# Two attention decode blocks on one core: every engine's program as a loop over one unit, with the score product written over the K tile

## The chip, the cores and the metric

The kernel runs on one core of a Trainium2 chip. The metric is the device time of one execution in microseconds, as a median of runs. The engines are TensorE (PE in the profile, with its weight loads as PEld), VectorE (DVE), ScalarE (ACT), GpSimd (POOL) and SyncE (SP), which issues the loads. A "q" behind an engine's name (PEldq, SPq) marks instructions of its queue: register arithmetic, branches, waits and the issue of transfers.

## The reference

Two independent blocks, A and B, of the same form and size. Each has one query token for each of 2 sequences:

```
q      = (x @ wq)                      # x: 2 x 1 x 640, wq: 640 x 6144, 32 heads of 192
scores = q . k_cache * 192 ** -0.5     # k_cache: 2 x 32 x 8192 x 192
p      = softmax(scores)               # over the 8192 keys
o      = p . v_cache                   # v_cache: 2 x 32 x 8192 x 192
out    = o @ wo                        # wo: 6144 x 640
```

The results of A and B are concatenated along the last axis. All data is bf16. The four caches are 805 MB; nearly all bytes are read once and used once.

## The kernel before

The work is cut into 64 units. A unit is a pair of neighbouring heads of one sequence of one block: a K tile and a V tile of 128 partitions x 24,576 bf16 elements (6.29 MB each). Partitions 0 to 63 hold the first head, 64 to 127 the second; a partition holds 128 keys of 192 numbers.

Three buffers in SBUF (`rings`, three slots of `RW` elements) take the tiles in the order K0, V0, K1, V1 and so on, each into the next slot. All loads go through SyncE's queue, in program order. A load waits until its slot is free: a K slot after the unit's fourth product (key `("m", i, 3)`), a V slot after the unit's V product (key `("pv", i)`); a V load waits for the V load before it too.

The steps of unit i:

- VectorE multiplies the K tile by the broadcast query, in four quarters of 32 keys each (`add_mul`, L322). The product goes to one of two buffers `prod`.
- TensorE sums each quarter's product over the 192 numbers in 12 steps of 16, as 12 accumulating matmuls with the identity (`add_sum`, L327), 128x512 into one of two PSUM banks `scps`; VectorE reduces the remaining 16 (`add_red`, L333) into the scores `sc`.
- VectorE takes each head's maximum per partition, GpSimd the maximum over partitions (L342), ScalarE the exponential (L354) into `pb`, with its sum in `rs`.
- TensorE multiplies the weights with the V tile: 64 accumulating matmuls of 34 weight columns by 384 (`add_pv`, L369), and sums `rs` over the partitions with a matmul (`add_l`, L382).
- In the next unit ScalarE and VectorE combine and normalise the two heads' output (`add_od`, `add_on`), and TensorE puts it into its place of the PSUM tile `oall` with 4 small matmuls (`add_place`, L410).
- TensorE broadcasts the query of the unit after next with one matmul (`add_q`, L309), and ScalarE copies it to `qt`, one of three buffers.
- TensorE also runs 12 matmuls on constant data per unit, whose results are not used (`add_fill`, L377).

Ahead of the units come the query projections: for each block 12 chunks of 512 columns, 5 matmuls each (`add_proj`, L291), from wq loaded in pieces into a slot and a `prod` buffer. Behind them comes the output projection: 48 rows per block (`add_contract`, L425), two matmuls a row, into partitions 0 and 32 of `outps`; the block A rows first, then its result is copied out, then block B. wo comes in 3 pieces (A) and 8 pieces (B).

The order on each engine is written out by hand: the class `_Stream` collects an engine's operations with what they wait for, and `loop` emits a stretch of them as a hardware loop. Before the change TensorE's unit is the body of one loop with 64 passes: 130 matmuls written out one after the other. VectorE and ScalarE have three units as a body, 21 passes. The projection is a loop of 6 passes for each block, two chunks a pass. SyncE and GpSimd have no loop. Semaphores count each engine's operations, so in a loop the value to wait for is worked out in a register (L112, L119). The V product's operand is the one of the large groups whose address comes from a register:

```python
at = slot * RW
if t is not None:
    at = eng.snap(((t * 2) % 3) * RW)
for j in range(T // 2):
    ins = eng.matmul(ops[0:34, 0:2 * Dh], pb[:, j, :], rings[:, bass.ds(at + j * (2 * Dh), 2 * Dh)],
                     start=(j == 0), stop=(j == T // 2 - 1))
```

Of the kernel before, what the change touches and what calls it, by code (L numbers as in the profile page):

```python
# [12 lines left out]
class _Stream:  # L13

    def __init__(self, name, sem, reg, first=0):
        self.name = name
        self.sem = sem
        self.reg = reg
        self.first = first
        self.count = first  # L20
        self.ops = []
        self.marks = []

    def add(self, fn, waits=(), sig=None):
        if sig is not None:
            self.count += 1
            assert sig not in self.reg, sig
            self.reg[sig] = (self.sem, self.count)
        self.ops.append((fn, tuple(waits), sig is not None))

    def mark(self):
        self.marks.append(len(self.ops))

    def needs(self, waits):
        need = {}
        for key in waits:
            if key is None or key[1:] and key[0] != "wo" and key[1] < 0 and key not in self.reg:
                continue
            sem, val = self.reg[key]
            sid = id(sem)  # L40
            if sid not in need or need[sid][1] < val:
                need[sid] = (sem, val)
        return need

    def run(self, eng, ops, waited):
        for fn, waits, has_sig in ops:
            for sid, (sem, val) in self.needs(waits).items():
                if val > waited.get(sid, 0):
                    eng.wait_ge(sem, val)  # L49
                    waited[sid] = val  # L50
            if fn is None:
                continue
            ins = fn(eng, None)
            if has_sig:
                ins.then_inc(self.sem, 1)

    def emit(self, eng, *loops, nc=None):
        waited, done = {}, 0
        if self.first:
            eng.sem_inc(self.sem, self.first)  # L60
        if nc is None:
            waited, done = self.rolled(eng, loops, waited, done)
            self.run(eng, self.ops[done:], waited)
            return
        names = [f"{self.name}_{x}" for x in ("main", "close", "end")]
        self.run(eng, self.ops[:1], waited)
        eng.br(names[0])
        marks, i0, step, n = loops[-1]
        with nc.body(names[1], valid_engines=[eng.engine]):
            self.run(eng, self.ops[marks[i0 + step * n]:], {})  # L70
            eng.br(names[2])
        with nc.body(names[0], valid_engines=[eng.engine]):
            self.rolled(eng, loops, waited, 1)
            eng.br(names[1])
        nc.switch_bb(names[2])

    def rolled(self, eng, loops, waited, done):
        for marks, i0, step, n in loops:
            at = [marks[i0 + step * t] for t in range(n + 1)]
            self.run(eng, self.ops[done:at[0]], waited)  # L80
            self.loop(eng, at, n, waited)
            waited, done = {}, at[n]
        return waited, done

    def loop(self, eng, at, n, waited):
        size = at[1] - at[0]
        passes = [self.ops[at[t]:at[t + 1]] for t in range(n)]
        needs = [[self.needs(w) for _, w, _ in ops] for ops in passes]
        delta = [{sid: needs[2][k][sid][1] - val for sid, (_, val) in need.items()} for k, need in enumerate(needs[1])]
        by, early = {}, {}  # L90
        for k, d in enumerate(delta):
            for sid, v in d.items():
                assert by.setdefault(sid, v) == v or not v or not by[sid]
                by[sid] = max(by[sid], v)
            for t, need in enumerate(needs):
                assert len(passes[t]) == size and passes[t][k][2] == passes[0][k][2]
                assert set(need[k]) == set(d) or t == 0 and set(need[k]) < set(d)
                for sid, (sem, val) in need[k].items():
                    plain = needs[1][k][sid][1] + (t - 1) * d[sid]
                    assert val == plain or t == 0 and val > plain  # L100
                    if val > plain:
                        early[sid] = (sem, max(val, early.get(sid, (sem, 0))[1]))
        for sid, (sem, val) in early.items():
            if val > waited.get(sid, 0):
                eng.wait_ge(sem, val)
                waited[sid] = val
        for k, need in enumerate(needs[1]):
            for sid, (sem, val) in need.items():
                if not delta[k][sid] and val > waited.get(sid, 0):
                    eng.wait_ge(sem, val)  # L110
                    waited[sid] = val
        with eng.Fori(0, n) as t:  # L112
            base = {sid: eng.snap(t * d) for sid, d in by.items() if d}
            waited = {}
            for k, (fn, _, has_sig) in enumerate(passes[0]):
                for sid, (sem, val) in needs[1][k].items():
                    at0 = val - delta[k][sid]
                    if delta[k][sid] and at0 > waited.get(sid, 0):
                        eng.wait_ge(sem, base[sid] + at0)  # L119
                        waited[sid] = at0  # L120
                    assert not delta[k][sid] or at0 > 0
                ins = fn(eng, t)
                if has_sig:
                    ins.then_inc(self.sem, 1)


def build_kernel(nc, blocks, out):
# [6 lines left out]
    NP = NBLK * B * PB  # L134
    LAST = NP - 1
    T = 128
    NB = 3
    STEP = 3
    LOOP = (1, STEP, 21)
    FIRST = 64  # L140
    TQ = T // 4
    DG = 16
# [3 lines left out]
    RW = T * Dh  # L146
    QC = 512
# [3 lines left out]
    WA = [(0, 19, 1, 0), (19, 38, 1, 19), (38, 48, 2, 0)]  # L151
    WB = [(0, 14, 2, 10), (14, 24, 2, 24), (24, 32, 0, 0), (32, 38, 0, 8), (38, 43, 0, 14), (43, 46, 0, 19),
          (46, 47, 0, 22), (47, 48, 0, 23)]

    def pair(i):
        blk, r = divmod(i, B * PB)
        b, ii = divmod(r, PB)
        return blk, b, ii

    with ExitStack() as es:  # L160
# [4 lines left out]
        qt = [sb(f"qt{i}", [128, Dh], BF16) for i in range(3)]  # L165
        sc = [sb(f"sc{i}", [128, T], F32) for i in range(NB)]
        filler = sb("filler", [128, 512], BF16)
        sb("spare", [128, 64], F32)
        rings = sb("rings", [128, 3 * RW], BF16)
        ring = [rings[:, i * RW:(i + 1) * RW] for i in range(3)]  # L170
        prod = [sb(f"prod{i}", [128, TQ * Dh], BF16) for i in range(2)]
        qrow = sb("qrow", [34, N], BF16)
        pb = sb("pb", [128, T // 2, 34], BF16)
        mp = [sb(f"mp{i}", [128, 2], F32) for i in range(NB)]
        mg = [sb(f"mg{i}", [128, 2], F32) for i in range(NB)]
        nb = [sb(f"nb{i}", [128, 1], F32) for i in range(NB)]
        rs = sb("rs", [128, 2], F32)
        rc = [sb(f"rc{i}", [2, 1], F32) for i in range(NB)]
        oodd = [sb(f"oodd{i}", [2, Dh], F32) for i in range(NB)]
# [4 lines left out]
        sel = sb("sel", [34, NBLK * B, 128], BF16)  # L184
        place = sb("place", [2, 264], BF16)
        ones = sb("ones", [128, 1], F32)
        oallS = [sb(f"oallS{k}", [128, WR, 2], BF16) for k in range(NBLK)]
        out_sb = [sb(f"out_sb{k}", [34, NH2], BF16) for k in range(NBLK)]
        actd = sb("actd", [128, 2], F32)
        warm = sb("warm", [128, 2], F32)  # L190

        scps = [ps(f"scps{i}", [128, TQ, DG], F32) for i in range(2)]
        ops = ps("ops", [128, 512], F32)
        pps = [ops, ps("pps", [128, 512], F32)]
        qps = ps("qps", [128, 512], F32)
        oall = ps("oall", [128, 512], F32)
        outps = ps("outps", [128, 512], F32)

        reg = {}
        S_sp = _Stream("sp", sem("s_sp"), reg)  # L200
        S_pe = _Stream("pe", sem("s_pe"), reg, FIRST)
        S_act = _Stream("act", sem("s_act"), reg, FIRST)
        S_dve = _Stream("dve", sem("s_dve"), reg, FIRST)
        PASS = [[], []]
        S_pool = _Stream("pool", sem("s_pool"), reg, FIRST)
        rsem = [sem(f"rsem{i}") for i in range(3)]
        psem = [sem(f"psem{i}") for i in range(2)]
        vsem = sem("vsem")
        xsem = sem("xsem")
        osem = [sem(f"osem{k}") for k in range(NBLK)]  # L210
        rcount = [0, 0, 0]

        def load(key, slot, out_ap, in_ap, waits):
# [387 lines left out]
```

## Time and profile before

| | |
|---|---|
| time, median of 3 runs | 1936.77 us (1936.73 to 1937.01) |
| span of the profiled execution, first to last instruction | 1935.5 us |
| busy: PE, DVE, ACT, POOL | 85%, 56%, 10%, 1% |
| DMA queue's share of 16 engines | 99.9% |
| read from HBM | 836.77 MB, 432 GB/s over the span |
| instructions | 26145 |

The profiled execution has no time of its own beside its span; the runs' median is 1.3 us above the span. In the profile a row of a group gives the line, the engine, the operation, the output and input tiles, the shapes, the count, then the busy time and the mean duration in ns, then the engine's idle time before these instructions with what ended it. A row of the timeline gives the start and the duration in us of a run of equal instructions. A row of one source line gives the shortest, median and longest duration in ns and the first and last start in us; the instructions of an engine's queue stand only there. "issue" is idle time in which the engine waited for nothing that the profile shows. A matmul's end is modelled, so rows of matmuls that follow closely overlap.

### The profile page before, as it was taken

How to read it: one execution, taken by the hardware profiler on the slowest of the kernel's cores; microseconds unless marked ns; L12 is line 12 of the kernel's file. 1: busy time of each engine (PE TensorE's matmuls, PEld its weight loads, DVE VectorE, ACT ScalarE, POOL GpSimd, SP SyncE). 2: the span in 40 equal slices, each digit the busy share in tenths (PEclk: the TensorE clock that was granted, in tenths of full speed). 3: DMA queues.
4: the chain of work that ended last, by engine and by line, in shares of the span. 5: the costliest groups of instructions: out<-in, count | busy, mean ns of one | idle time of the engine just before them, and what ended most of it. 6: DMA issues, size and time to landing. Idle time of an engine off the chain costs nothing.

```text
span 1935.5 us, 26145 instructions
## 1 busy us (share of the span) xinstructions
PE 1637.3 (85%) x8653; PEld 791.5 (41%) x8718; DVE 1081.5 (56%) x837; ACT 188.2 (10%) x612; POOL 28.6 (1%) x86
## 2 busy tenths in 40 slices
PE   4888888888888888888888888888888888888888
PEld 1344443443443443443443443443443443443444
DVE  0556646646656646646656646646656646646652
ACT  2111011011011011011011011011011001001000
POOL 1000000000000000000000000000000000000000
PEclk9999999999999999999999999999999999999999
DMA  9999999999999999999999999999999999999999
GB/s 421 431 430 439 435 428 438 437 428 436 437 429 435 438 431 432 439 435 428 438 435 431 435 437 431 433 439 434 429 438 435 430 436 436 431 434 438 431 433 392
DMA packets 20768, 836.87 MB, mean 432 GB/s; under 512 B 2316, under 2 KB 2584, under 8 KB 3096
## 3 DMA queue, kind: packets, MB, share of 16 engines
q1 hardware_dynamic: 20752, 836.78, 99.9%
q8 instruction: 3, 0.05, 0.0%
q14 instruction: 5, 0.04, 0.0%
q10 hardware_dynamic: 8, 0.00, 0.0%
HBM read 836.77 MB, written 0.01 MB: 432 GB/s over the span
## 4 chain that ended last, share of the span: by engine, by line
issue 92%; DMA 3%; PE 3%; POOL 1%; DVE 1%; ACT 0%; SPq 0%; POOLq 0%; DVEq 0%; ACTq 0%
DMA rings<-in_B_wq_dram 2%; POOL mg L342 1%; PE ops L369 1%; DMA rings<-in_B_wo_dram 1%; DVE prod L322 1%; PE scps L327 1%; PE ops L291 0%; PE pps L291 0%; SPq L219 0%; DVE sc L333 0%; ACT pb L354 0%; POOLq L49 0%; ACT qrow L297 0%; DVE mp L339 0%; ACT out_sb L433 0%
## 5 line engine op out<-in xcount | busy, mean ns | idle before, releaser
L322 DVE TENSOR_TENSOR prod<-rings,qt 128x6144 bf16<-128x6144 bf16 x256 | 852.8, 3352 | 698.6 <-DMA rings<-in_B_k_cache_dram 332.3
L327 PE MATMUL scps<-prod,ident 128*128 128x512 bf16 x3072 | 708.7, 381 | 193.5 <-DVE prod L322 193.5
L369 PE MATMUL ops<-rings,pb 128*34 x4096 | 676.5, 326 | 4.9
L327 PEld LDWEIGHTS scps<-prod,ident 128*128 128x128 bf16 x3072 | 280.3, 98 | 598.6 <-DVE prod L322 293.0
L369 PEld LDWEIGHTS ops<-rings,pb 128*34 128x34 bf16 x4096 | 399.4, 98 | 263.7 <-issue 11.2
L333 DVE TENSOR_REDUCE sc<-scps 128x32 f32<-128x512 f32 x256 | 175.7, 686 | 109.2 <-PE scps L327 109.2
L377 PE MATMUL outps<-filler,ident 128*128 128x512 bf16 x704 | 162.4, 379 | 10.2 <-issue 10.2
L377 PEld LDWEIGHTS outps<-filler,ident 128*128 128x128 bf16 x768 | 69.9, 98 | 77.9
L386 ACT ACTIVATE oodd<-ops 2x192 f32<-2x192 f32 x64 | 20.6, 322 | 699.4 <-PE ops L369 699.4
L315 ACT ACTIVATE qt<-qps 64x192 bf16<-64x192 f32 x66 | 21.4, 324 | 670.1 <-PE qps L309 670.1
L354 ACT ACTIVATE pb<-sc,nb 64x128 bf16<-64x128 f32 x128 | 81.5, 636 | 8.0
L382 PE MATMUL ops<-ones,rs 128*2 128x1 f32 x128 | 12.1, 164 | 58.4 <-ACT pb L354 58.4
L342 POOL PARTITION_ALL_REDUCE mg<-mp x64 | 22.8, 356 | 1871.7 <-DVE mp L339 1871.7
L347 ACT ACTIVATE nb<-mg 64x1 f32<-64x1 f32 x64 | 13.0, 203 | 307.9 <-POOL mg L342 307.9
L382 PEld LDWEIGHTS ops<-ones,rs 128*2 128x2 f32 x128 | 5.5, 82 | 90.0 <-ACT pb L354 90.0
L354 ACT ACTIVATION_READ_ACCUMULATOR pb<-sc,nb 64x1 f32 x128 | 38.4, 300 | 0.0
L309 PE MATMUL qps<-qrow,sel 34*128 (+1 forms) x66 | 22.0, 333 | 1.4 <-ACT qt L316 0.8
L410 PEld LDWEIGHTS oall<-on,place 2*128 x260 | 10.5, 92 | 28.6 <-issue 27.1
L338 DVE TENSOR_REDUCE mp<-sc 64x1 f32<-64x128 f32 x64 | 17.8, 278 | 7.9
L316 ACT ACTIVATE qt<-qps 64x192 bf16<-64x192 f32 x66 | 21.5, 326 | 0.8
L392 DVE TENSOR_TENSOR oodd<-ops,oodd 2x192 f32<-2x192 f32 x64 | 20.8, 326 | 0.2 <-ACT oodd L386 0.2
L394 DVE TENSOR_SCALAR on<-oodd,rc 2x192 bf16<-2x192 f32 x64 | 19.7, 307 | 2.3
(53 smaller groups left out, 165.7 us busy)
## 6 DMA issues: line engine op xcount, KB each, us to landing
rings<-in_A_k_cache_dram SPq DMA_DIRECT2D x32, 6144.0 KB, 26.1
rings<-in_A_v_cache_dram SPq DMA_DIRECT2D x32, 6144.0 KB, 28.9
rings<-in_B_k_cache_dram SPq DMA_DIRECT2D x32, 6144.0 KB, 26.1
rings<-in_B_v_cache_dram SPq DMA_DIRECT2D x32, 6144.0 KB, 28.9
rings<-in_A_wq_dram SPq DMA_DIRECT2D x1, 6144.0 KB, 20.7
rings<-in_B_wq_dram SPq DMA_DIRECT2D x1, 6144.0 KB, 37.5
rings<-in_A_wo_dram SPq DMA_DIRECT2D x2, 3040.0 KB, 22.3
rings<-in_B_wo_dram SPq DMA_DIRECT2D x1, 2240.0 KB, 23.2
```

The lines of the kernel that those rows point to most:

```text
L309: return eng.matmul(qps[:, 0:2 * Dh], sel[:].rearrange("p s m -> p (s m)")[:, bass.ds(k, 128)], qrow[:, bass.ds(c, 2 * Dh)], start=True, s ...
L315: eng.activation(qt[i % 3][0:64, :], qps[0:64, 0:Dh], ACTF.Identity)
L316: return eng.activation(qt[i % 3][64:128, :], qps[64:128, Dh:2 * Dh], ACTF.Identity)
L322: S_dve.add(lambda eng, t: eng.tensor_tensor(pr3(qd), quarter(i, qd), q, ALU.mult), waits=w, sig=("m", i, qd))
L327: ins = eng.matmul(scps[qd % 2][:], ident[:], pr3(qd)[:, :, j * DG:(j + 1) * DG], start=(j == 0), stop=(j == NJ - 1))
L333: S_dve.add(lambda eng, t: eng.tensor_reduce(sc[i % NB][:, qd * TQ:(qd + 1) * TQ], scps[qd % 2][:], AXL.X, ALU.add), waits=[("s", i, qd), ...
L342: S_pool.add(lambda eng, t: eng.partition_all_reduce(mg[i % NB][:], mp[i % NB][:], 128, bass.bass_isa.ReduceOp.max), waits=[("mx", i), key ...
L354: ins = eng.activation(pb[p0:p0 + 64, :, h::32], sc[i % NB][p0:p0 + 64, :].rearrange("p (j a) -> p j a", a=2), ACTF.Exp, bias=nb[i % NB][p ...
L369: ins = eng.matmul(ops[0:34, 0:2 * Dh], pb[:, j, :], rings[:, bass.ds(at + j * (2 * Dh), 2 * Dh)], start=(j == 0), stop=(j == T // 2 - 1))
L377: ins = eng.matmul(to, ident[:], filler[:], start=True, stop=True)
L386: S_act.add(lambda eng, t: eng.activation(oodd[i % NB][:], ops[32:34, Dh:2 * Dh], ACTF.Identity), waits=[("pv", i), key("on", i - NB)], si ...
L392: S_dve.add(lambda eng, t: eng.tensor_tensor(oodd[i % NB][:], ops[0:2, 0:Dh], oodd[i % NB][:], ALU.add), waits=[("od", i)], sig=("ad", i))
```

## The change

The class `_Stream` goes. Each engine has a program written out with loops, and the order of the steps in a unit stays nearly as it was.

- **Loops.** All of TensorE's, VectorE's, ScalarE's, GpSimd's and SyncE's programs have one unit as body, 64 passes (SyncE: one V load and one K load, in loops of 30 and 31 passes). TensorE's unit has loops of its own: 4 quarters, in each of them 4 passes of two matmuls with 4 matmuls outside; 12 passes of one filler matmul; 16 passes of four V matmuls. The projection has one chunk a pass, the output projection one row a pass, with a wait in each. Operands in the ring, in `pb`, in `scps` and in `oallS` are addressed from registers.
- **Product over the K slot.** VectorE writes the product where the K tile is; `prod` goes. The K slot is free for the next V load after the unit's fourth sum (semaphore `su`), no longer after its fourth product.
- **Slots** are `SW` = 30,720 elements apart, so that a whole wq or half of wo fits. wq comes in one load per block, A's wo in one load (before: three), B's in eight.
- **One accumulation for the output.** `oallS` holds four columns for each of the 96 rows, two of them zero, and the rows of both blocks accumulate into the same two PSUM banks, partitions 0 to 3. Two engines copy them out, two queues store them. Two matmuls with a zero operand open and close the V product's accumulation, as the loop's body can't carry the flags.
- **Single buffers** for `sc`, `qt`, `mp`, `mg`, `nb`, `rc`, `oodd`. The query is broadcast one unit ahead instead of two, and copied after the unit's exponential.
- A helper `hold` waits on a semaphore and then counts up another; GpSimd passes on the arrival of wq and wo to TensorE.

The diff, cut to its core:

```diff
-        prod = [sb(f"prod{i}", [128, TQ * Dh], BF16) for i in range(2)]
-        rings = sb("rings", [128, 3 * RW], BF16)
+        rings = sb("rings", [128, 3 * SW], BF16)
...
+        def program_sync(eng):
+            for blk in range(NBLK):
+                w = blocks[blk]["wq"].rearrange("(j c) n -> j (c n)", c=DC)
+                eng.dma_start(slot(blk, SW), w).then_inc(Z[f"wq{blk}"], 16)
...
+            load("k", 0, 0, 2)
+            eng.wait_ge(Z["pr"], NQC)
+            load("v", 0, 0, 0)
+            eng.wait_ge(Z["pr"], 2 * NQC)
+            eng.wait_ge(Z["ks"], 16)
+            load("k", 0, 128, 1)
...
+                hold(eng, "vs", w16)
+                hold(eng, "su", w4)
+                load("v", blk_v, v0, sv)
...
+                hold(eng, "ks", k16)
+                hold(eng, "pv", w1)
+                load("k", blk_k, k0, sk)
...
+                def mul(q):
+                    k3 = rings[:, bass.ds(at + q * QW, QW)].rearrange("p (t d) -> p t d", d=Dh)
+                    eng.tensor_tensor(k3, k3, q3, ALU.mult).then_inc(Z["mu"], 1)
...
+                with eng.Fori(0, NQC) as t:
+                    eng.wait_ge(Z["qe"], eng.snap(k * NQC + t + 1))
+                    to, at = eng.snap((t & 1) * 512), eng.snap(k * SW + t * QC)
+                    for c in range(DC):
+                        ins = eng.matmul(pflat[0:4, bass.ds(to, QC)], xT[:, c, :],
+                                         rings[:, bass.ds(at + c * N, QC)], start=(c == 0), stop=(c == DC - 1))
...
+            with eng.Fori(0, NP) as t:
+                u = eng.snap(t + 1)
+                with eng.Fori(0, 4) as q:
+                    n = eng.snap(t * 4 + q + 1)
+                    at = eng.snap(((t * 2 + 2) % 3) * SW + q * QW)
+                    to = eng.snap((q & 1) * 512)
+                    eng.wait_ge(Z["mu"], n)
+                    eng.wait_ge(Z["re"], n)
...
+                    one(at, True)
+                    one(at + DG, False)
+                    with eng.Fori(0, NJ // 2 - 2) as j:
+                        at_j = eng.snap(at + j * (2 * DG))
+                        one(at_j + 2 * DG, False)
+                        one(at_j + 3 * DG, False)
+                    one(at + (NJ - 2) * DG, False)
+                    ins = one(at + (NJ - 1) * DG, False, True)
+                    ins.then_inc(Z["su"], 1)
+                eng.wait_ge(Z["qtd"], u)
+                make_q(u)
+                n = eng.snap((t + (NP - 1)) & (NP - 1))
+                eng.wait_ge(Z["on"], u)
+                put(eng.snap((n & (3 * PB)) * (WR // PB)), eng.snap((PB - (n & (PB - 1))) * 8)).then_inc(Z["pl"], 1)
+                with eng.Fori(0, 12) as _:
+                    eng.matmul(fps[:], ident[:], filler[:], start=True, stop=True)
+                eng.wait_ge(Z["ex"], u)
+                eng.wait_ge(Z["vs"], eng.snap(u * 16))
+                eng.matmul(ops[0:PW, 0:2 * Dh], zero[:], filler[:, 0:2 * Dh], start=True, stop=False)
...
+                with eng.Fori(0, T // 8) as g:
+                    aj, vj = eng.snap(g * (4 * PW)), eng.snap(g * (4 * 2 * Dh) + sv)
+                    for j in range(4):
+                        eng.matmul(ops[0:PW, 0:2 * Dh], pflat2[:, bass.ds(aj + j * PW, PW)],
+                                   rings[:, bass.ds(vj + j * (2 * Dh), 2 * Dh)], start=False, stop=False)
+                eng.matmul(ops[0:PW, 0:2 * Dh], zero[:], filler[:, 0:2 * Dh], start=False, stop=True)
+                eng.matmul(ops[0:2, 448:449], rs[:], ones[:], start=True, stop=True).then_inc(Z["pv"], 1)
...
+            with eng.Fori(0, NR - PIECES[-1]) as r:
+                eng.wait_ge(Z["wo"], eng.snap(r + 1))
+                contract(r, False, False)
```

In it `one` is a sum's matmul, which takes its operand from the ring at the register's offset and writes to one of the two banks of `scps`, `put` the four matmuls of place, and `contract` a row's two matmuls.

More of the change, by code (lines that the diff above doesn't have):

```diff
@@ L10 @@
 F32 = mybir.dt.float32
[L13 to L124, printed above, removed]
```

594 lines of the change are left out of this document (264 added, 330 removed).

## The prediction

> **What bounds the kernel now.** I read the page's first, third and fourth parts first: which engine or queue is full.
>
> ```profile
> span 1935.5 us, 26145 instructions
> PE 1637.3 (85%) x8653; PEld 791.5 (41%) x8718; DVE 1081.5 (56%) x837; ACT 188.2 (10%) x612; POOL 28.6 (1%) x86
> ...
> q1 hardware_dynamic: 20752, 836.78, 99.9%
> ...
> HBM read 836.77 MB, written 0.01 MB: 432 GB/s over the span
> issue 92%; DMA 3%; PE 3%; POOL 1%; DVE 1%; ACT 0%; SPq 0%; POOLq 0%; DVEq 0%; ACTq 0%
> ```
>
> The transfers fill 99.9% of the span: the bound is the DMA, and no byte of the 836.77 MB goes away. TensorE has 15% left, so it is second. The chain of waits names nearly nothing but "issue" and is no help. Then one unit (one pair of heads) in the timeline, where the next two rows of a kind give the period.
>
> ```profile
> 1012.20 6.63 DVE L322 TENSOR_TENSOR prod<-rings,qt 128x6144 bf16<-128x6144 bf16 x2 [10.42 <-DMA rings<-in_B_k_cache_dram]
> 1015.00 0.33 SPq L219 DMA_DIRECT2D rings<-in_B_k_cache_dram  x1
> 1015.61 2.76 PE L327 MATMUL scps<-prod,ident 128*128 128x512 bf16 x12 [0.65 <-DVE prod L322]
> ...
> 1023.21 3.35 DVE L322 TENSOR_TENSOR prod<-rings,qt 128x6144 bf16<-128x6144 bf16 x1
> ...
> 1026.61 2.76 PE L327 MATMUL scps<-prod,ident 128*128 128x512 bf16 x12 [0.84 <-DVE prod L322]
> 1026.71 0.33 SPq L219 DMA_DIRECT2D rings<-in_B_v_cache_dram  x1
> ...
> 1029.41 0.69 DVE L333 TENSOR_REDUCE sc<-scps 128x32 f32<-128x512 f32 x1 [1.60 <-PE scps L327]
> 1029.73 2.54 PE L377 MATMUL outps<-filler,ident 128*128 128x512 bf16 x11 [0.16 <-issue]
> ...
> 1033.16 0.19 PE L382 MATMUL ops<-ones,rs 128*2 128x1 f32 x2 [0.88 <-ACT pb L354]
> 1033.41 10.57 PE L369 MATMUL ops<-rings,pb 128*34 x64
> 1041.36 6.63 DVE L322 TENSOR_TENSOR prod<-rings,qt 128x6144 bf16<-128x6144 bf16 x2 [10.56 <-DMA rings<-in_B_k_cache_dram]
> ```
>
> From K landing to K landing, 1012.20 to 1041.36, is 29.16 us: two tiles of transfer, 14.58 each. TensorE's own work in it: four sums of 2.76, q and place about 0.6, filler 2.59, V product 10.57 and 0.19, together about 25. So it may grow by some 4 us a unit before it takes the bound over. A sum issues one matmul per (2.76 - 0.38) / 11 = 0.216, the V product one per (10.57 - 0.33) / 63 = 0.163 (a lone matmul shows 0.38 and 0.33).
>
> Last the instructions of TensorE's own queue, which count as busy nowhere and show only when a source line is asked for: the loop (L112), one pass's end, the V product's addresses (L369) at its start and its end, those of place (L410), a lone wait (L49). Columns: count, ns least/median/most, first and last start.
>
> ```profile
> L112 PEldq ALU_OP  x76: 32/32/32, 24.2 to 1911.5; - x76
> L112 PEldq COMPARE_BRANCH  x76: 76/213/237, 24.3 to 1911.6; - x76
> ...
> L112 PEldq ALU_OP  x1: 32/32/32, 1070.8 to 1070.8; - x1
> L112 PEldq FUSED_REGOPS  x1: 50/50/50, 1071.1 to 1071.1; - x1
> ...
> L369 PEldq FUSED_REGOPS  x11: 46/46/106, 1033.3 to 1034.6; - x11
> ...
> L369 PE MATMUL ops<-rings,pb x25: 326/326/326, 1010.7 to 1014.6; 128*34 x25
> L369 PEldq FUSED_REGOPS  x12: 46/46/46, 1011.0 to 1012.4; - x12
> ...
> L410 PEldq FUSED_REGOPS  x5: 46/46/68, 1028.2 to 1028.8; - x5
> L410 PEldq ALU_OP  x4: 32/36/36, 1027.9 to 1028.4; - x4
> L410 PEldq MOVE  x1: 29/29/29, 1028.1 to 1028.1; - x1
> ...
> L49 PEldq EVENT_SEMAPHORE  x4: 51/51/51, 55.2 to 1923.1; - x4
> ```
>
> Four prices follow. Ten register instructions of place stand between 1027.9 and 1028.8: 0.1 each, 0.09 without the three matmuls issued among them, so some 0.06 lies between two. A register instruction with its weight load and matmul: eleven in 1.3, 0.13 (weight load and matmul add 0.03). A pass's end is a count and a jump: 0.032 + 0.06 + 0.213 + 0.06 = 0.36, and 1070.8 to 1071.1 agrees; the last pass, which falls through (76), costs 0.23. A separate wait: 0.11. Before the change none of it is seen: 0.13 is below the 0.163 of a V matmul, the queue ends its addresses at 1012.4 when the last matmul starts at 1014.6, and there is one pass end a unit.
>
> **The change, part by part.** PE's unit becomes a nest of short loops: 4 quarters with 4 inner passes of two matmuls each, 12 passes of one filler matmul, 16 passes of four V matmuls. That is 49 pass ends a unit with the outer one, where there was 1. Every operand in the ring, and pb's too, gets an address from a register. In us, by the prices above:
> - A quarter: some five register instructions for its count, slot and bank 0.5; a second wait 0.11; two matmuls 0.26; the inner counter 0.09; four passes of 2 x 0.13 + 0.36, less 0.13: 2.35; two matmuls 0.26; its end 0.36. Together 3.9, where the matmuls alone need 2.6. Four: 15.5.
> - q and place: 15 register instructions as now, 1.5.
> - Filler: 12 x (0.03 + 0.36) = 4.6, where the matmuls need 2.6.
> - Waits for exp and V: 0.5.
> - V product: per matmul two addresses. If both are made in one register instruction, it is a little over 0.13: 0.14; if in two, 0.22. The trace decides neither, but one such instruction does hold several steps: the slot's doubling, remainder and product with the first address is the 106 ns one of L369. I take 0.14. The first of a pass, which makes two pass offsets too, 0.23. A pass is 0.23 + 3 x 0.14 + 0.36 = 1.01, where the matmuls need 0.65. Sixteen, with the two matmuls by zero and the row sum: 16.4.
> - Unit's end and counters: 0.5.
>
> The sum is 39.0 us per unit. Nothing hides it: each stage is issued slower than the array works, so the array waits for its queue. Against 29.16 the DMA loses the bound. What else of the unit is late then? Exp is ready some 2.2 after the maximum (1030.9 to 1033.16 now), before the fillers end; VectorE's four products and sums, 3.35 + 0.6 each, fit in 15.5; so both are covered.
>
> Other edits of the unit. The product over the K slot frees that slot after the last sum (1029.4) instead of the last product (1026.6). V's load is queued at 1026.71 for a transfer that starts at 1041.36, so 2.8 later costs nothing; K's (queued 1015.00, starts 26.36 - 14.58 = 11.8 later) still follows the V product. At 39 a unit both have 10 more. Single sc, qt, mp, nb: their reuse waits on work a third of a unit old, nothing. In place the product may cost VectorE more or less; the nearest row is its 3.35, and it is covered up to some 0.1 per quarter; I take nothing. SP's register steps and extra waits, under 1 us a load, lie in the same slack.
>
> Start. The q projection now has one chunk a pass: some six register instructions 0.5, five matmuls 0.65, end 0.36, less what the array's lead covers, about 1.3 against the 1.08 shown here.
>
> ```profile
> 33.71 1.03 PE L291 MATMUL ops<-rings,xT 128*2 x4
> ...
> 34.78 1.03 PE L291 MATMUL pps<-rings,xT 128*2 x4
> ...
> 57.63 6.63 DVE L322 TENSOR_TENSOR prod<-rings,qt 128x6144 bf16<-128x6144 bf16 x2 [53.42 <-ACT qt L316]
> ```
>
> wq in single loads moves the same bytes; the second block's 12 chunks end 12 x 0.22 = 2.6 later, so the first product starts near 60.2 and its sums at 63.6. The first unit also waits for VectorE; it ends near 105.
>
> End. The output accumulation runs 95 rows in passes of two matmuls, into the same partitions one after the other. Now:
>
> ```profile
> 1915.94 6.68 PE L425 MATMUL outps<-rings,oallS 128*2 128x320 bf16 x96 [0.46 <-ACT oallS L416]
> ...
> 1933.33 0.08 PEld L425 LDWEIGHTS outps<-rings,oallS 128*2 128x2 bf16 x2 [0.32 <-DMA rings<-in_B_wo_dram]
> 1933.67 0.43 ACT L433 ACTIVATE out_sb<-outps 34x320 bf16<-34x320 f32 x1 [10.57 <-PE outps L425]
> ```
>
> A pass: the wait's value 0.09, three addresses in two instructions 0.22, matmul 0.03, one more 0.13, end 0.36: 0.83. 95 of them 79 us. The wo loads (two of 7.86 MB, 18 us each at 432 GB/s) are issued from the last unit's start and middle, and are in SBUF before. From the V product's end (1913.98) to the first row (1915.94) is 2.0 now, 2.6 with more register work; 1933.33 to the span's end is 2.2, and stays.
>
> Sum: 105 + 63 x 39.0 = 2562; + 2.6 + 79 + 2.2 = 2646. Outside the span lie 1936.77 - 1935.5 = 1.3. About **2650 us**, 37% slower.
>
> **The rivals.**
> - *Two instructions for a V matmul's addresses* (0.22 for 0.14): 64 x 0.09 = 5.8 more a unit, x 64 = 371: 3020. For it: place shows a separate register instruction for each different address.
> - *The jump is cheaper in a short loop.* All 76 here close loops of ten matmuls or more. Its floor is the compare that falls through, 76 ns: 0.137 less on each of 42 jumps a unit, some of it taken back by the array's pace: 33.8 a unit, 13 less at the end: about 2310. Against it: loops of 10 and of 130 matmuls share the same median. [...]
> - *The queue runs ahead and hides the passes.* It decides at (29.16 - 25) / 49 = under 0.09 us per pass, a quarter of what a pass end shows. Then the DMA stays the bound and the time is 1937 if the last rows keep up, 1945 if each row's two matmuls follow one another (95 x 0.27 = 26 from 1915.9, against a last landing at 1933.3). For it: the lead of 2.2 us at 1012.4. Against: a lead grows only where the array is slower than its queue, and every stage starts from a wait. [...]
> - *The clock falls*, since the array is busy for only two thirds of the time.
>
> ```profile
> 1018.90:1029.00 10.10, 8.16 (x37) 3.35 (x37) 8.88 (x8) 0.65 (x2) 0.00 (x0) 1.00 1.06 457
> 41.00:45.30 4.30, 4.22 (x12) 1.38 (x13) 0.00 (x0) 0.81 (x2) 0.00 (x0) 0.60 0.84 366
> ```
>
> It fell to 0.60 after 3 us of nothing (second row), not with 12 matmuls per 3.87 us (first row, clock 1.00), which is as dense as the new V product. At half speed sums and V product go by the array, 47.5 a unit: 3180.
>
> **How the numbers follow.** The sum as it stands 0.60, two instructions 0.18, cheap jump 0.09, clock 0.07, hidden passes 0.06. The range reaches from the cheap jump to the two instructions, 2300 to 3030, and leaves out clock and hidden passes, 0.13, and a little of the edges. A measurement tells 0.2% (4 us) from no change: slower 0.97, same 0.02 and faster 0.01, both out of the hidden passes.
>
> **What would show it.** The DMA share near 0.75, and K landings 39 us apart. PE idle "issue" in front of L-rows of filler and V product; twelve fillers over 4.6 us, 64 V matmuls over 16, twelve of a sum over 3. COMPARE_BRANCH some 3250 times (49 x 64, 26 and 95) with a median near 210. The output rows over 79 us. VectorE's product still 3.35. Wrong would be V matmuls at 0.163 throughout, a compare under 0.1, or a period of 29.

## The result, and the profile after

The changed kernel takes 2993.32 us (median of 6 runs, 2991.91 to 3032.74) against 1936.88 (6 runs of the kernel before beside them). The means of the runs have a ratio of 1.549, 95% interval 1.543 to 1.554. The profiled execution has a span of 2990.8 us and a time of 2992.3.

The page of the changed kernel, its parts one, three and four:

```profile
span 2990.8 us, 40096 instructions
...
PE 2203.1 (74%) x8838; PEld 823.6 (28%) x8838; DVE 1099.4 (37%) x840; ACT 187.5 (6%) x610; POOL 28.8 (1%) x86
...
q1 hardware_dynamic: 20030, 836.78, 67.9%
...
PE 74%; issue 21%; DVE 4%; DMA 1%; ACT 0%; SPq 0%; ACTq 0%; DVEq 0%
```

The same 836.77 MB now fill 68% of the span. In the chain, TensorE (74%) and "issue" (21%) stand where "issue" alone stood: the queue of TensorE has become the bound. The timeline of one unit shows it. The columns are start, length, engine, line, names, shape, count and the idle time of the engine before.

```profile
1503.07 0.33 PE L333 MATMUL qps<-qrow,sel 36*128 x1 [0.27 <-issue]
...
1504.32 4.65 PE L373 MATMUL fps<-filler,ident 128*128 128x512 bf16 x12
...
1508.92 0.33 PE L376 MATMUL ops<-filler,zero 128*34 128x384 bf16 x1
...
1509.44 0.82 PE L382 MATMUL ops<-rings,pb 128*34 x4 [0.19 <-issue]
...
1510.66 0.82 PE L382 MATMUL ops<-rings,pb 128*34 x4 [0.40 <-issue]
...
1528.87 0.19 PE L385 MATMUL ops<-ones,rs 128*2 128x1 f32 x2
...
1530.04 3.72 PE L356 MATMUL scps<-rings,ident 128*128 x12 [0.98 <-issue]
...
1533.80 0.69 DVE L230 TENSOR_REDUCE sc<-scps 128x32 f32<-128x512 f32 x1 [19.70 <-PE scps L356]
...
1534.48 3.70 PE L356 MATMUL scps<-rings,ident 128*128 x12 [0.72 <-DVE sc L230]
...
1543.39 3.74 PE L356 MATMUL scps<-rings,ident 128*128 x12 [0.72 <-issue]
...
1547.44 0.33 PE L333 MATMUL qps<-qrow,sel 36*128 x1 [0.31 <-issue]
```

From one q (1503.07) to the next (1547.44) is 44.37 us, and nothing in it waits for a transfer. The twelve fillers take 4.60 and a pass of four V matmuls 1.21 to 1.25; the array works for 0.82 of that and is idle for 0.4 "issue". The four sums come 4.45 apart although twelve matmuls need 2.6. One attribution is not to be believed: the second sum's idle time is put down to VectorE's reduction, but that reduction ends at 1533.80 + 0.69 = 1534.49, and the sum starts at 1534.48. What ends last there is TensorE's own queue.

Its instructions, by source line (count, ns least/median/most, first and last start): the V loop (L379), its matmuls' addresses (L382), the start of a pass of a sum (L360) and of a quarter (L346).

```profile
L379 PEldq FUSED_REGOPS  x16: 193/193/193, 1509.1 to 1527.5; - x16
...
L379 PEldq COMPARE_BRANCH  x16: 76/208/208, 1510.0 to 1528.5; - x16
```
```profile
L382 PEldq FUSED_REGOPS  x64: 60/74/79, 1509.3 to 1528.2; - x64
```
```profile
L360 PEldq FUSED_REGOPS  x1024: 145/145/155, 66.8 to 2876.4; - x171
```
```profile
L346 PEldq FUSED_REGOPS  x256: 110/110/115, 61.5 to 2873.1; - x128
```

The jump is what was forecast (208 ns, 76 where it falls through). Where the forecast took some 46 ns for nearly every register instruction, the trace has longer kinds: 74 for a matmul with two addresses, 110, 145 and 193 where a loop's counter and the slot are turned into an address, and one of up to 189 in each quarter (L356).

Unit ends, the first and the last (the row sum's line, 109.7 to 2903.8), are 63 periods of 44.35 apart; then come the output rows.

```profile
L385 PE MATMUL ops<-ones,rs x128: 163/164/165, 109.7 to 2903.8; 128*2 128x1 f32 x128
```
```profile
2906.61 2.34 PE L398 MATMUL pps<-rings,oallS 128*4 x6
...
2986.16 2.06 PE L398 MATMUL pps<-rings,oallS 128*4 x6 [0.18 <-issue]
```

### The profile page after: what moved, and what is told of

Read it like the earlier page. It is cut to its first block, busy times and chain, and to the rows that moved or that the text cites. A ratio compares the mean times of both kernels' runs of the same rounds, so it can differ in the third digit from the quotient of the medians.

```text
span 2990.8 us, 40096 instructions
## 1 busy us (share of the span) xinstructions
PE 2203.1 (74%) x8838; PEld 823.6 (28%) x8838; DVE 1099.4 (37%) x840; ACT 187.5 (6%) x610; POOL 28.8 (1%) x86
## 3 DMA queue, kind: packets, MB, share of 16 engines
HBM read 836.77 MB, written 0.01 MB: 280 GB/s over the span
## 4 chain that ended last, share of the span: by engine, by line
PE 74%; issue 21%; DVE 4%; DMA 1%; ACT 0%; SPq 0%; ACTq 0%; DVEq 0%
PE scps L356 29%; PE ops L382 28%; PE fps L373 10%; DVE sc L230 4%; PE pps L398 2%; PE oall L338 1%; PE pps L324 1%; PE qps L333 1%; PE ops L376 1%; DMA xr<-in_B_x_dram 1%; PE ops L384 0%; PE ops L385 0%; DVE rings L226 0%; ACT qrow L262 0%; PE pps L402 0%
## 5 line engine op out<-in xcount | busy, mean ns | idle before, releaser
L382 PE MATMUL ops<-rings,pb 128*34 x4096 | 840.7, 328 | 394.9 <-issue 391.5
L356 PE MATMUL scps<-rings,ident 128*128 x3072 | 863.8, 384 | 297.2 <-DVE sc L230 128.4
L226 DVE TENSOR_TENSOR rings<-rings,qt 128x6144 bf16 x256 | 852.8, 3352 | 267.5 <-ACT qt L268 267.5
L382 PEld LDWEIGHTS ops<-rings,pb 128*34 x4096 | 382.1, 93 | 850.4 <-issue 659.6
L356 PEld LDWEIGHTS scps<-rings,ident 128*128 128x128 bf16 x3072 | 293.9, 96 | 849.0 <-issue 799.7
L373 PE MATMUL fps<-filler,ident 128*128 128x512 bf16 x768 | 306.8, 447 | 2.9
L373 PEld LDWEIGHTS fps<-filler,ident 128*128 128x128 bf16 x768 | 74.8, 97 | 206.8 <-issue 204.7
L398 PE MATMUL pps<-rings,oallS 128*4 x192 | 66.3, 449 | 15.3 <-issue 8.5
L338 PE MATMUL oall<-on,place 2*128 2x48 bf16 x260 | 37.4, 189 | 27.2 <-issue 26.1
L324 PE MATMUL pps<-rings,xT 128*4 x120 | 32.0, 405 | 6.5 <-issue 5.7
```

Source lines behind the costliest of these rows:

```text
L226: eng.tensor_tensor(k3, k3, q3, ALU.mult).then_inc(Z["mu"], 1)
L324: ins = eng.matmul(pflat[0:4, bass.ds(to, QC)], xT[:, c, :], rings[:, bass.ds(at + c * N, QC)], start=(c == 0), stop=(c == DC - 1))
L338: ins = eng.matmul(oall[:, bass.ds(sec, WR)], place[:, bass.ds(at - a, 128)], on[:, a * WR:(a + 1) * WR], start=False, stop=False)
L356: return eng.matmul(sflat[:, bass.ds(to, 512)].rearrange("p (t g) -> p t g", g=DG), ident[:], src, start=start, stop=stop)
L373: eng.matmul(fps[:], ident[:], filler[:], start=True, stop=True)
L382: eng.matmul(ops[0:PW, 0:2 * Dh], pflat2[:, bass.ds(aj + j * PW, PW)], rings[:, bass.ds(vj + j * (2 * Dh), 2 * Dh)], start=False, stop=False)
```

## The experiments

Each runs beside the kernel before (1936.8 to 1936.9 in all of them). "Unit" is from one place in a unit to the same place in the next. Theory Q, mine, is that the unit is the sum of TensorE's steps, each paced by its queue.

**V product written out** (`v_straight`).

```diff
-                with eng.Fori(0, T // 8) as g:
-                    aj, vj = eng.snap(g * (4 * PW)), eng.snap(g * (4 * 2 * Dh) + sv)
-                    for j in range(4):
-                        eng.matmul(..., pflat2[:, bass.ds(aj + j * PW, PW)], rings[:, bass.ds(vj + j * (2 * Dh), 2 * Dh)], ...)
+                for j in range(T // 2):
+                        eng.matmul(..., pflat2[:, j * PW:(j + 1) * PW], rings[:, bass.ds(sv + j * (2 * Dh), 2 * Dh)], ...)
```

> The changed kernel with its V product written out: 64 matmuls, pb at fixed addresses, only the ring address in a register. Theory Q (TensorE's unit is the sum of its steps, each paced by the queue's register, counter and jump instructions): the V product falls from 19.2 us to 64 x 0.163 = 10.4, the unit from 44.4 to 35.6, the time by 64 x 8.8 = 560 to about 2430 us; V matmuls 0.163 apart. Theory B (single buffers and the product over the K slot: the unit waits on the round between VectorE and TensorE over the sums, which the page names with 128 us in front of the sums): TensorE comes to its sums 8.8 us earlier and waits there for VectorE, the time stays above 2900. Theory C (the array or its clock sets the pace of the V matmuls): 19 us and 2990 stay.

Measured: 2285.1 us (2272.3 and 2297.9), further down than theory Q's 2430. The timeline:

```profile
1511.44 10.57 PE L381 MATMUL ops<-rings,pb 128*34 x64
...
1521.85 0.33 PE L383 MATMUL ops<-filler,zero 128*34 128x384 bf16 x1
...
1522.10 0.19 PE L384 MATMUL ops<-ones,rs 128*2 128x1 f32 x2
...
1522.22 2.76 PE L356 MATMUL scps<-rings,ident 128*128 x12
...
1525.39 3.74 PE L356 MATMUL scps<-rings,ident 128*128 x12 [0.41 <-issue]
```

The V product takes 10.41, as expected. The rest is in the rows behind it: the first sum starts 0.12 after the row sum, where it was 1.17, and the second sum 3.17 after it, where it was 4.44. In this product the address instructions of the queue start from 1511.3 to 1519.4 (0.13 each), the matmuls from 1511.4 to 1521.7 (0.163 each). So at the end of the 64 the queue is 2.3 us ahead, and by 1522.2 it has the quarter's start and its first passes behind it. 8.76 + 0.34 (before the product) + 1.05 + 1.27 = 11.4 a unit, 731 us; 708 were measured, 720 between the profiled runs. So here a written-out stage also pays for the short loop that follows it. The granted clock has a part in the rest: 26 units of this trace, in each of which it falls to 0.50 for 3.4 us, are 33.27 long on the mean, the others 32.93, which is the 11.4 less than 44.35. Theories B and C fall.

**The inner loop of a sum written out** (`sum_straight`).

```diff
-                    with eng.Fori(0, NJ // 2 - 2) as j:
-                        at_j = eng.snap(at + j * (2 * DG))
-                        one(at_j + 2 * DG, False)
-                        one(at_j + 3 * DG, False)
+                    for j in range(2, NJ - 2):
+                        one(at + j * DG, False)
```

> The changed kernel with the inner loop of a sum written out (12 matmuls in a row), the loop over the quarters kept. Theory Q: twelve matmuls at 0.22 and a quarter's own 1 us of queue work make 3.5 us a quarter in place of 4.45; the last quarter then waits for VectorE's last product (product and reduction alternate, 3.35 + 0.69 each), so the four take about 14.2 in place of 17.4; 64 x 3.2 = 205 less, about 2790 us. Theory B: the idle time put to the reduction is a true wait, so the sums keep 17.4 a unit and the time stays at 2990.

Measured: 2750.6 us (2738.7 and 2762.5). The timeline of the four sums, with the q matmul behind them:

```profile
1521.51 5.42 PE L356 MATMUL scps<-rings,ident 128*128 x24 [0.94 <-issue]
...
1524.92 3.35 DVE L226 TENSOR_TENSOR rings<-rings,qt 128x6144 bf16 x1
...
1528.85 2.76 PE L356 MATMUL scps<-rings,ident 128*128 x12 [1.92 <-DVE rings L226]
...
1535.41 0.33 PE L333 MATMUL qps<-qrow,sel 36*128 x1
```

Two sums run through in 5.42 and the third waits 1.92 for VectorE's product. Here the named release bears checking: the product ends at 1524.92 + 3.35 = 1528.27, and the sum starts 0.6 later, after the rest of the quarter's queue work. The four sums take 13.90 for 17.40, q and place 0.5 less: 64 x 4.0 = 256, and 254 were measured between the profiled runs. This second bound, VectorE's round (a reduction, then the next product, in the order of its program; the products start 3.87 apart), is why the four sums can't get under 13.5 to 13.9 here.

**The filler written out, and left out** (`filler_straight`, `no_filler`).

```diff
-                with eng.Fori(0, 12) as _:
+                for _ in range(12):          # filler_straight; range(0) in no_filler
```

> The changed kernel with the twelve filler matmuls written out. Theory Q: 4.6 us become 12 x 0.216 = 2.6; the exponentials are ready 2.2 after the first filler matmul, so all of it counts: 64 x 2.0 = 128 less, about 2865 us. Theory B: the V product waits for something else (exponentials, V's landing), and the time stays within 20 us of 2993.

> The changed kernel without the twelve filler matmuls of a unit (they feed nothing). Theory Q: 4.6 us go from TensorE's queue, but the exponentials are ready only 2.2 after the place where the fillers began; so the V product starts about 2.4 earlier: 64 x 2.4 = 152 less, about 2840 us, with the idle time before it put to ACT. Rival (clock): the array then stands idle for more than 2 us in each unit, its clock falls under 0.9, and the time stays above 2900.

Measured: 2861.8 us (2846.8 and 2876.8) and 2844.2. In the two timelines:

```profile
1515.81 2.76 PE L373 MATMUL fps<-filler,ident 128*128 128x512 bf16 x12
...
1518.50 0.34 PE L376 MATMUL ops<-filler,zero 128*34 128x384 bf16 x1
```
```profile
1513.54 0.33 PE L333 MATMUL qps<-qrow,sel 36*128 x1 [0.30 <-issue]
...
1517.04 0.33 PE L376 MATMUL ops<-filler,zero 128*34 128x384 bf16 x1 [2.22 <-ACT pb L288]
```

Written out, the fillers take 2.69 for 4.60, and the step behind them 0.18 for 0.52. Left out, from q to the product is 3.50 where it was 5.85, with 2.22 idle put down to the exponentials: 64 x 2.35 = 150, measured 149. The fillers' loop costs its difference to the exponentials' readiness, not its length. The granted clock was 0.93 on the mean for 0.97, not under 0.9, and the time is under 2900: the clock rival falls.

**What a V pass is made of** (`v_pbfix`, `v_8x8`, `v_ind`, `ind`). First one of the two addresses fixed, then eight matmuls a pass:

```diff
-                        eng.matmul(ops[0:PW, 0:2 * Dh], pflat2[:, bass.ds(aj + j * PW, PW)],   # v_pbfix
+                        eng.matmul(ops[0:PW, 0:2 * Dh], pflat2[:, j * PW:(j + 1) * PW],
-                with eng.Fori(0, T // 8) as g:                                                # v_8x8
+                with eng.Fori(0, T // 16) as g:      # with g * (8 * ...) and 8 matmuls
```

> The changed kernel with the V product's loop kept, but pb always read at its first four columns' fixed addresses, so a matmul takes one address from a register and a pass makes one offset (this leaves out the right weights). Theory Q: the excess of a V pass over the forecast (1.23 us for 1.01) lies in the register instructions that make two values at once (193 ns for a pass's two offsets, 74 for a matmul's two addresses); with one value each I expect near 106 and 46, a pass of 1.03, 16 x 0.2 = 3.2 less per unit, about 2790 us. Rival: what counts is the number of register instructions, which stays (one a matmul, one a pass): 2990.

> The changed kernel with the V product in 8 passes of 8 matmuls, not 16 of 4. Theory Q: a pass is 0.25 for its offsets, 0.155 a matmul, 0.36 for its end; eight passes fewer save 8 x 0.61 = 4.9 a unit, 64 x 4.9 = 312, about 2680 us. Rival (the addresses of the matmuls set the pace, the jump is cheap or hidden): 16 passes of 1.23 are then 64 x 0.3, and the time stays within 60 us of 2990.

Measured: 2877.6 and 2681.3 us. Queue rows of the first, timeline of the second:

```profile
L382 PEldq FUSED_REGOPS  x51: 46/46/46, 1500.7 to 1543.5; - x51
```
```profile
L379 PEldq FUSED_REGOPS  x18: 193/193/193, 1500.3 to 1544.0; - x18
```
```profile
1514.20 1.47 PE L382 MATMUL ops<-rings,pb 128*34 x8 [0.39 <-issue]
1516.04 1.47 PE L382 MATMUL ops<-rings,pb 128*34 x8 [0.37 <-issue]
```

With one address the instruction of three of a pass's four matmuls falls from 74 to 46 ns, the first one's from 60 to 36, and the loop's counter from 36 to 32: 0.112 x 16 x 64 = 115, and 2993.3 - 2877.6 is 115.7. The instruction of 193 ns stays, so my reading that it is long because it makes two offsets was wrong. A pass of eight takes 1.84, as forecast from 0.25 + 8 x 0.155 + 0.36; eight passes fewer save 312.0, forecast 312.

What makes the 193 then? The slot of V is the remainder (2t) % 3 times the slot's length; it is written once ahead of the loop, but no register instruction stands there in the trace. So in the next kernel the loop counts the address itself:

```diff
-                with eng.Fori(0, T // 8) as g:
-                    aj, vj = eng.snap(g * (4 * PW)), eng.snap(g * (4 * 2 * Dh) + sv)
+                eng.reg_mov(pbat, 0)
+                with eng.Fori(sv, sv + (T // 2) * 2 * Dh, 4 * 2 * Dh) as vj:
+                    aj = eng.snap(pbat, min_val=0, max_val=(T // 2 - 4) * PW)
...
+                    eng.reg_add(pbat, pbat, 4 * PW)
```

and `ind` has the same in the inner loop of a sum (`eng.Fori(at + 2 * DG, at + (NJ - 2) * DG, 2 * DG) as at_j`).

> The changed kernel, V product still 16 passes of 4, but the loop counts the ring address itself (from the slot's start in steps of a pass) and pb's address is a register that one addition moves on; nothing is left to be worked out at the start of a pass. Theory Q2: the 193 ns instruction of a pass is the slot's remainder and product, worked out anew in each pass, and with the 0.06 behind it costs 0.25; a 36 ns addition costs 0.1: 16 x 0.15 = 2.5 less a unit, 64 x 2.5 = 158, about 2835 us. Rival: the pass's start is covered by the jump before it or the weight loads, the time stays at 2990.

> As the kernel before it in this list, and the inner loop of a sum counts its ring address itself too (the 145 ns instruction at the start of a pass goes). Theory Q2: 0.2 to 0.25 a pass, sixteen passes a unit; the sums come down from 17.4 to the 13.5 to 14.2 that VectorE's products allow: 3.2 to 3.9 a unit, 205 to 250 less, about 2600 us. Rival (only the count of passes matters): as the one before, near 2835.

Measured: 2777.7 and 2692.2 us. The V product of the first, and the register row of a sum's loop in the second:

```profile
1525.66 0.82 PE L384 MATMUL ops<-rings,pb 128*34 x4
1526.66 0.84 PE L384 MATMUL ops<-rings,pb 128*34 x4 [0.18 <-issue]
...
1541.47 0.33 PE L387 MATMUL ops<-filler,zero 128*34 128x384 bf16 x1
```
```profile
L361 PEldq FUSED_REGOPS  x45: 42/50/73, 1500.3 to 1543.7; - x45
```

A pass goes from 1.23 to 1.00 (0.99 on the mean of sixteen), more than the 0.15 expected: the pass's 193 ns and the first matmul's 60 have become one instruction of 74, and the addition (51 ns) replaces the loop's own counter (36). The product takes 15.81 for 19.17, 64 x 3.36 = 215, measured 215.6. An instruction of 143 ns now stands once in a unit, ahead of the loop. So the remainder was worked out again in every pass. In the sums I expected 3.2 to 3.9 a unit, and 1.34 came: the quarters are 4.13 apart for 4.45. The 145 ns instruction did go, but instructions of some 50 ns stand in its place, and I had priced these at nothing.

**All inner loops written out, and all but the filler's** (`all_straight`, `all_but_filler`): the edits above together, the quarters and the output rows written out too. The outer loop, the product over the K slot, the single buffers, the single loads and the loops of the other engines stay.

> The changed kernel with all of TensorE's inner loops written out (quarters, sums, filler, V product, output rows); the outer loop over the units stays, and so do the product over the K slot, the single buffers, the single loads, the loop of the transfers' queue and those of the other engines. Theory Q: the loops of TensorE's queue are the whole loss; the unit needs about 10.4 + 2.6 + 13.9 + 3 = 29.9 by VectorE's round at most and 29.2 by the DMA, so 1937 to 1985 us with a DMA share above 0.97. Theory B: the other parts of the change cost by themselves; the unit stays above 33 and the time above 2150 us.

> As the kernel with all of TensorE's inner loops written out (1951 us), but the twelve fillers in their loop again: 2.0 us more on TensorE's queue per unit. The prediction gave TensorE 4 us of slack under the DMA's 29.16, by its busy time: then 1951 stays. The chain of the unit (place 0.7, filler 4.6, V product 10.4 with 0.6 around it, and four sums that VectorE's products pace at 13.9, not 4 x 2.76) gives 30.2 a unit: about 110 + 63 x 30.2 + 31 = 2040 us, with the DMA no longer full.

Measured: 1951.27 us, ratio 1.0074 (1.0057 to 1.0091), and 1996.45 us, 1.031 (1.025 to 1.037). The first zero matmul of a unit, the start of its sums, its q, and the next unit's zero matmul, in both:

```profile
1500.77 0.33 PE L375 MATMUL ops<-filler,zero 128*34 128x384 bf16 x1 [0.63 <-ACT pb L288]
...
1512.22 2.76 PE L357 MATMUL scps<-rings,ident 128*128 x12 [0.42 <-DVE rings L226]
...
1525.86 0.33 PE L333 MATMUL qps<-qrow,sel 36*128 x1
...
1529.72 0.33 PE L375 MATMUL ops<-filler,zero 128*34 128x384 bf16 x1 [0.63 <-ACT pb L288]
```
```profile
1511.89 0.33 PE L375 MATMUL ops<-filler,zero 128*34 128x384 bf16 x1 [4.71 <-issue]
...
1522.85 5.35 PE L357 MATMUL scps<-rings,ident 128*128 x24
...
1536.31 0.33 PE L333 MATMUL qps<-qrow,sel 36*128 x1
...
1541.56 0.33 PE L375 MATMUL ops<-filler,zero 128*34 128x384 bf16 x1 [4.68 <-issue]
```

Written out, 1042 of the 1056 us are back. The unit is 28.95, and TensorE waits in two places: 0.63 ahead of the V product, for the exponentials, and 0.42 ahead of the sums, for VectorE's product, which waits for K's landing. With the filler's loop q to V takes 5.25 without a wait, where it took 3.86 with 0.63 of waiting in it: TensorE's work grows by 2.02, but the unit only by 0.72, to 29.67. The wait for the exponentials took up 0.63; the other 0.67 went into the time up to the sums (10.96 from the zero matmul for 11.45) and into the sums (13.46 for 13.64). 63 x 0.72 = 45, which is the 45.2 measured. The 0.67 shows in the first kernel by itself, too: its first units, whose K lies there early, are 28.29 long, 0.67 under the later 28.96. I had expected 30.2 a unit and 2040, with the sums at 13.9; they took 13.46.

**What is left to the kernel before** (`all_straight_halves`, `all_straight_halves_proj`). In the kernel written out, the rows of the output, and the DMA's share in the one us in which the second V load is issued, at 82.22 (columns: window, length, busy times, clock, DMA share, GB/s):

```profile
1920.29 27.86 PE L396 MATMUL pps<-rings,oallS 128*4 128x320 bf16 x192
```
```profile
82.00:83.00 1.00, 0.83 (x7) 0.57 (x8) 0.95 (x3) 0.00 (x0) 0.00 (x0) 1.00 0.01 0
```

The rows end at 1948.2, some 12 us behind the last transfer (1936), and near 82 us nothing moves. The first edit puts the two halves into different partitions, the second writes the q projection out as well.

```diff
-                    ins = eng.matmul(pps[0:4, h, 0:NH2], lhs, rhs, start=start, stop=stop)
+                    ins = eng.matmul(pps[32 * h:32 * h + 4, h, 0:NH2], lhs, rhs, start=start, stop=stop)
...
-                with eng.Fori(0, NQC) as t:                                    # ..._proj
+                for t in range(NQC):
```

> As the kernel with all inner loops written out (1951 us), but the two halves of the output accumulated in partitions 0 to 3 and 32 to 35 rather than both in 0 to 3. Theory R: there 192 matmuls into the same four partitions follow one another at 0.146 us, 28 us from 1920.3, 14 us past the last landing; into two sets of partitions they go at 0.07 (the kernel before shows 6.68 for 96), 13.4 us, and end with the last landing near 1934: about 1938.5 us. Rival: the number of columns streamed sets the pace whatever the partitions: 1951 stays.

> As the one before it, with the q projection written out too. The DMA had a hole of 2.4 us near 80 us: the second V load waits for the first unit's last sum (81.7), since the product stands in K's slot, and that sum is late by the looped projection (60.7 for 57.6). Theory H: written out, the first product starts some 4 us earlier, the load is queued ahead of the landing at 79.8, the hole goes: 2 to 3 us less, 1936 to 1937 us, within 0.2% of the kernel before. Rival (the single load of wq or the loop of the transfers' queue costs it): 1938.5 stays.

Measured: 1941.47 us, 1.0024 (1.0014 to 1.0033), and 1938.30 us, 1.0008 (0.9999 to 1.0017). The second one's rows and its V load (its transfers fill 99.9% of the span):

```profile
1917.30 13.61 PE L396 MATMUL pps<-rings,oallS 128*4 128x320 bf16 x172
...
1932.97 1.08 PE L396 MATMUL pps<-rings,oallS 128*4 128x320 bf16 x10 [0.28 <-POOLq L197]
```
```profile
76.68 0.37 SPq L116 DMA_DIRECT2D rings<-in_A_v_cache_dram  x1
```

172 row matmuls take 13.61, 0.079 each for 0.145, and then wait for their last pieces. In the first edit, which changes nothing else about these matmuls, 144 of them take 9.95, 0.069 each: their partitions set that pace here, not the 320 columns; what in the array makes it so was not shown. The load is issued at 76.68, ahead of the landing, and 3.2 us come back. Not all of it is the load's: of the 3.9 us between the two profiled runs 2.7 stand at the last row sum (1917.48 and 1914.80). The rest lies in the last rows, where 20 matmuls of the first took 2.64 with the granted clock falling to 0.50; the second kept 1.00. 1938.5 and 1936 to 1937 had been expected: 3 and 1 to 2 too little. The rest of the change (product over the slot, single buffers, single loads, transfers' loop) then costs next to nothing: the interval still holds 1.000 and ends at 0.17%, though all eleven runs (from 1937.84) lie above all twenty of the kernel before (to 1937.19), with 1.4 us between the medians. No version here beats the kernel before; it is at 99.9% of the DMA too.

## Why the forecast held, and where it was off

The forecast was 2650 us in a range of 2300 to 3030; 2993 lies at the upper edge of it. The mechanism was right: TensorE's queue takes the bound, and writing its loops out takes nearly all of it back. The likeliest value was 343 too low. By its steps, in us a unit:

| step | forecast | measured | rows |
|---|---|---|---|
| q and place | 1.5 | 1.25 | 1503.07 to 1504.32 |
| filler | 4.6 | 4.60 | 1504.32 to 1508.92 |
| waits and V product | 16.9 | 19.95 | 1508.92 to 1528.87 |
| unit's end and four quarters | 16.0 | 18.57 | 1528.87 to 1547.44 |
| unit | 39.0 | 44.37 | |

- *V product*: the step that failed is "the first of a pass, which makes two pass offsets too, 0.23". These offsets are an instruction of their own, 193 ns and 0.06 behind it, and the first matmul has its address besides. The other three go at 0.155, not 0.14 (74 ns for 46): a pass is 1.23 for 1.01. I had read from before's trace that a slot's remainder costs 106 ns once a unit; that it is worked out again in every pass `v_ind` showed.
- *Quarters*: the passes "of 2 x 0.13 + 0.36" have no term for the 145 ns at the start of each, and come 0.71 apart for 0.62. The quarter's start, counted with "some five register instructions" at 0.5 and a wait at 0.11, has one of 110 and one of up to 189 ns in it and takes 0.81. A quarter is 4.45 for 3.9.
- *Two instructions for a V matmul's addresses* (3020) gave nearly the measured time for the wrong reason: each matmul has one instruction, in 64 of 64 cases. (0.22 for 0.14 is 0.08 and not 0.09 a matmul, so its sum should have been some 2980.) The range's upper end, 3030, was taken from this rival; that 2993 lies inside is partly luck.
- *Jump*: about 210 forecast, 208 measured, in loops of one, two and four matmuls. The cheap-jump rival falls.
- *Filler*: right to 0.05.
- *VectorE's product in place*: 3.352 for 3.35, over 256 of them. Right.
- *Start and end*: the first unit ends at 109.9, not 105 (the projection has 1.46 a chunk for 1.3, the quarters and V as above); rows 82 us for 79.
- *TensorE may grow by 4 us a unit*: wrong. I added up busy time, four sums of 2.76; but VectorE's products pace them at 13.5 to 13.9. `all_but_filler` put the room at 1.3 for the fillers, and at 0.67 for work that the wait for the exponentials doesn't cover. It changes little here, where the unit grows by 15; an edit of 2 us a unit it would have called free, and that one cost 45 us. The queue that hides its passes (1937 to 1945), the rival that leaned on this room, falls by the first rows above: the array idles for "issue" ahead of every V pass.
- *The clock falls*: for short stretches in some units, and throughout the output rows.

```profile
1502.00:1548.00 46.00, 33.78 (x138) 12.70 (x136) 17.91 (x15) 2.65 (x9) 0.35 (x1) 1.00 0.66 274
2908.00:2988.00 80.00, 64.73 (x189) 15.11 (x188) 0.00 (x0) 0.00 (x0) 0.00 (x0) 0.50 0.00 0
```

The third number from the end is the granted clock. In the unit shown, with rests of 0.2 to 1.0 us, it is 1.00. In 25 of the units before 1200 us it is 0.50 for 3.4 us (from 1197 to 1199, for one, where the fillers take 5.00 for 4.60 and the next V passes make it up); these units are 44.35 long like the others. Its price shows in `v_straight`, 0.34 in each of 26 units, 9 us. In the output rows, two matmuls per 0.86, it is 0.50 throughout; what it costs there was not tried, but the queue's part of a row was forecast at 0.83.

Left open: the instructions of a quarter were not priced one by one as those of a V pass were, and what the product over the K slot or a single buffer costs in a kernel whose units have less room was not tried.

## What to carry over

Here a loop on TensorE's queue added to its work where its pass was longer in the queue than on the array: 1.23 for 0.65 (four at 0.163) in a V pass, 0.38 for 0.22 in the filler. Count per pass the jump (0.27 with its gap here), the counter, and every address, with the arithmetic written into it, and hold it against the pass's work. Room on an engine is read from the waits in its unit, not from busy time; here they leave 0.67 us, and 0.63 more ahead of the V product, not 4. Where a loop has to stay, let it count the address itself, and put as many matmuls into a pass as fit: eight for four gave back 312 us.

## What the hardware showed that I had not expected

Register instructions are not of one price: 36, 46, 74, 110, 145 and 193 ns in one kernel. Where it was tried, the one that holds more arithmetic took longer: 74 with two addresses, 46 with one (`v_pbfix`); 193 with the slot's remainder at the start of a pass, 74 without it (`v_ind`). And the queue carried its lead over a stage's border: after 64 V matmuls written out, the next short loop ran 1.27 us faster without any edit of its own.
